# The bound of |v| as ScalarE sums in place of VectorE maxima, and column halves for the 90-row scores

## Chip, core and metric

The kernel runs on one core of a Trainium2 chip. The metric is device time in microseconds (us) of the whole program, less is better. The engines are TensorE (PE; PEld is its weight load), VectorE (DVE), ScalarE (ACT), GpSimd (POOL) and SyncE (SP), which issues most DMAs.

## What is computed

An attention with mixed heads, and a gated layer on its output. There are 4 batches, 12 heads, 448 tokens and a head width of 64; the layer has 1792 tokens, width 768 and an inner width of 1536.

```python
scores = scale * np.matmul(q, k.transpose(0, 1, 3, 2))
scores = np.einsum('bhij,hg->bgij', scores, w_pre)
scores = scores - np.max(scores, axis=-1, keepdims=True)
attn = np.exp(scores)
attn = attn / (np.sum(attn, axis=-1, keepdims=True) + 1e-09)
attn = np.einsum('bhij,hg->bgij', attn, w_post)
out = np.matmul(attn, v)
...
gate = 1.0 / (1.0 + np.exp(-(x @ w_gate)))
return gate * (x @ w_val) @ w_out
```

## The kernel before

The attention comes first, and the layer (the MoE part of the code) follows it. Queries are cut into blocks of 120, 120, 120 and 88 rows for each batch; the last is taken as 90 rows, since heads are mixed in sets of 10 rows. Two sets make a unit, and there are 92 units. The code is written out slot by slot, one slot for each unit, and every engine takes its instructions in that order.

In slot s, TensorE does, in this order: `premix` of unit s+2 (`pm`, L211), one `scores` call of a later block (`qk`, L157), `postmix` of unit s (`mx`, L253), and a part of `av` (L280, attention times v). ScalarE does the exponential of the first set (`e`, L223, an ACTIVATE and a read of its accumulator), the copy of one score tile (`st`, L163), the second exponential, then `mix` (L261, which empties the one `mx` buffer in PSUM, so that the `postmix` of slot s+1 waits for it), and in some slots `xt` (L290) or a sum over weights (L989). VectorE does a reciprocal (`ss`, L229, which waits for `ss` from GpSimd, L228), two row maxima (`nm`, L216), the other copy of the scores (L163), two `pl` (L241), and then what the plan adds to the slot. GpSimd does `ss`, two `ph` (L235), and in many slots a conversion of weights (L1067, L1075). Three slots take two `scores` calls, the second one at the slot's end: 13, 36 and 59, each just after six 90-row calls.

`scores` multiplies 64 rows of q and k for two heads, one head in each half of the array's rows. For a block of 120 query rows it cuts the columns at 64, so that four matmuls (each of them two instructions, for f32) have a quarter of the array each. For the 90-row blocks there is no cut. These are 6 calls for each of the four batches, 24 in all, in slots 7 to 12, 30 to 35, 53 to 58 and 76 to 81.

The layer scales its operands by powers of two, and needs a bound of |x|. It is the largest bound of |v| times the largest row sum of |w_post|. `v_max` (L175) gives one column of `vm` for each batch and head, by a VectorE reduction over 256 values in each partition; there are 48 of them, 12 for each batch, one for each slot from the batch's slot 6 on, with slots left out (`taken`) in which other VectorE work stands. `v_bound` (L181, L182 and the transpose L999) combines them after every second batch, and its result goes through SP's queue as `max_x`.

Of the kernel before, what the change touches and what calls it, by code (L numbers as in the profile page):

```python
# [9 lines left out]
F32 = mybir.dt.float32  # L10
F32R = mybir.dt.float32r
F16 = mybir.dt.float16
BF16 = mybir.dt.bfloat16
# [3 lines left out]
AF = mybir.ActivationFunctionType  # L17
ALU = mybir.AluOpType
AX = mybir.AxisListType
# [6 lines left out]
QUAD = 4  # L26
# [15 lines left out]
def _attention(ctx, tc, ins, B, H, S, D, xs, raws, make_moe):  # L42

    nc = tc.nc
# [11 lines left out]
    const = ctx.enter_context(tc.tile_pool(name="a_const", bufs=1))  # L56
# [32 lines left out]
    w2lo = const.tile([128, HK], F16, name="w2lo")  # L89
    sw = const.tile([128, 1], F32, name="sw")  # L90
    iw = const.tile([128, 1], F32, name="iw")
    vm = const.tile([128, B * H], F32, name="vm")
    vr = const.tile([128, 1], F32, name="vr")
    wr = const.tile([128, 1], F32, name="wr")
    wc = const.tile([128, H], F32, name="wc")
# [30 lines left out]
    moe = make_moe(NG)  # L126
# [23 lines left out]
    def scores(bi, c, sc):  # L150
        b, n = blocks[bi][0], R * blocks[bi][4]
        q, k = q_t[bi], k_t[b, c]
        cuts = [(0, 64), (64, n)] if n > 96 else [(0, n)]
        for s0, s1 in cuts:
            for e in range(2):
                rows = slice(64 * e, 64 * e + 64)
                nc.tensor.matmul(sc[e][s0:s1, :S], lhsT=q[rows, c, s0:s1], rhs=k[rows, :], start=True, stop=True)  # L157
# [8 lines left out]
    vt = {}  # L166
# [4 lines left out]
        vt[b, u] = t  # L171


    def v_max(b, h):
        nc.vector.tensor_reduce(vm[:, H * b + h:H * b + h + 1], vt[b, h // QUAD][:, h % QUAD].rearrange("p j d -> p (j d)"),  # L175
                                axis=AX.X, op=ALU.max, apply_absolute_value=True)

    def v_bound(b, step):
        g = "x", b // 2
        if step == 0:  # L180
            nc.vector.tensor_reduce(vr, vm[:, 2 * H * g[1]:2 * H * (g[1] + 1)], axis=AX.X, op=ALU.max)  # L181
            nc.vector.tensor_scalar(moe.one[("top",) + g], vr, wr, 1.001, op0=ALU.mult, op1=ALU.mult)  # L182
            stores.append(moe.flipped(g))
        else:
            moe.early_bound(g, step + 1)
# [112 lines left out]
    EARLY_AT = (5, 12, 19, 27, 34, 42, 49, 57)  # L298
# [3 lines left out]
    def at(slot, fn, *args):  # L302
        plan.setdefault(slot, []).append((fn, args))

    def spread(i, n, s0, s1):
        return s0 + i * (s1 - s0) // n

    taken = {EARLY_AT[k] + slot for k in range(moe.EARLY) for slot in (10, 11)}
    for b in range(B):
        f = first[PB * b]  # L310
        for u in range(NQ):
            at(f + 2 + 2 * u, v_load, b, u)
        s = f + 5
        for h in range(H):
            s = max(s + 1, f + 6 + 2 * (h // QUAD))
            while s in taken:
                s += 1
            at(s, v_max, b, h)
        if b % 2:
            at(s + 1, v_bound, b, 0)  # L320
        if b == 1:
            for step, slot in enumerate(BOUND[1:]):
                at(s + 1 + slot, v_bound, b, step + 1)
        for c in range(NP if b else 0):
            at(spread(c, NP, first[PB * (b - 1)] + 6, first[PB * b - 1] - LEAD - 2), k_load, b, c)
    for bi in range(1, NBK):
        s0, s1 = first[bi - 1] - LEAD, first[bi] - LEAD
        for c in range(NP):
            at(spread(c, NP, s0, s1), scores, bi, c)
        if bi > 1:  # L330
            at(s0 - 4, q_load, bi)
    for bi in range(NBK):
        s0 = first[bi + 1]
        s1 = first[bi + 2] if bi + 2 < len(first) else s0
# [39 lines left out]
    def ahead(c):  # L374
        if c % 3 == 0:
            mx = two_banks(ps_mx, "mx")
            sc = [mx[:, e] for e in range(2)]
        else:
            sc = pm[:2] if c % 3 == 1 else qk_banks()
        scores(0, c, sc)  # L380
        todo.append(sc)
# [14 lines left out]
    for s in range(min(min(plan), -LEAD), max(plan) + 1):  # L396
# [14 lines left out]
        def job(bi, c):  # L411
            sc = qk_banks()
            scores(bi, c, sc)
            return lambda e: keep(bi, c, e, sc)
# [785 lines left out]
@with_exitstack  # L1200
def kernel(ctx, tc, B, H, S, D, ins, out):
    nc = tc.nc
    top = ctx.enter_context(tc.tile_pool(name="top", bufs=1))
    dram = ctx.enter_context(tc.tile_pool(name="dram", bufs=1, space=DRAM))
    xs = dram.tile([B, H * D // 128, 128, S], F32, name="xs")
    with tc.manual_schedule():
        raws = top.tile([128, 13 * H * D // 2], F32, name="raws")
        with ExitStack() as c2:
            moe = _attention(c2, tc, ins, B, H, S, D, xs, raws,
                             lambda NG: _Moe(tc, xs, ins, out, raws, NG, top))  # L1210
        moe.run()
# [72 lines left out]
```

## Time and profile before

| what | value |
|---|---|
| median of 3 runs | 789.11 us (788.37 to 790.18) |
| profiled execution, first to last instruction (span) | 786.5 us |
| the median less that span | 2.6 us |
| mean granted TensorE clock | 0.998 |
| PE, DVE, ACT, POOL busy | 97%, 83%, 70%, 37% of the span |

The profiled execution's own time is given as its span; the 2.6 us beside it are the start and end of the program. The attention takes about the first 344 us. A slot is counted below from the first `mx` matmul of its unit to that of the next, so slot 8 is the stretch from 50.02 to 53.48 us.

### The profile page before, as it was taken

What the parts mean: (1) busy time and instruction counts of PE and PEld (TensorE: products, weight loads), DVE (VectorE), ACT (ScalarE), POOL (GpSimd) and SP (SyncE); (2) the same over time, 40 slices, a digit from 0 to 9 for tenths busy, and PEclk for the clock granted to TensorE, in tenths of its full rate; (3) what the DMA queues carried; (4) which work ended last, traced back from release to release, by engine and by line L of the source; (5) the groups of instructions that cost most, each with busy time, mean ns of one, the idle gap of its engine ahead of it and who ended that gap; (6) DMA issues with size and microseconds to landing.
All of it is one profiled execution on the core that took longest, in us unless ns stands there. A gap on an engine that the chain in (4) does not pass through costs nothing.

```text
span 786.5 us, 23288 instructions
## 1 busy us (share of the span) xinstructions
PE 760.4 (97%) x9530; PEld 417.6 (53%) x9530; DVE 649.4 (83%) x1116; ACT 548.3 (70%) x1058; POOL 293.7 (37%) x462
## 2 busy tenths in 40 slices
PE   7899999999999999888999999999999999999998
PEld 2455655565556555564555455555555555555554
DVE  4999999999989999999996989589876999997111
ACT  3887889788978888796875876577756784563000
POOL 1447776876786544410222222224222221010000
PEclk9999999999999999999999999999999999999999
DMA  5786568756875575839406284663567788995001
GB/s 183 232 255 223 192 231 260 252 193 227 284 261 186 183 226 186 250 105 321 143 27 224 92 301 152 251 222 141 198 205 263 277 313 312 383 346 206 36 36 70
DMA packets 80714, 166.13 MB, mean 211 GB/s; under 512 B 20448, under 2 KB 57664, under 8 KB 80608
## 3 DMA queue, kind: packets, MB, share of 16 engines
q1 hardware_dynamic: 72304, 132.88, 51.0%
q0 software_dynamic: 7728, 31.27, 10.3%
q8 instruction: 74, 1.21, 0.7%
q10 hardware_dynamic: 576, 0.51, 0.2%
q14 instruction: 32, 0.26, 0.1%
HBM read 87.77 MB, written 38.15 MB: 160 GB/s over the span
## 4 chain that ended last, share of the span: by engine, by line
PE 77%; ACT 9%; DVE 7%; DMA 3%; POOL 2%; issue 2%; SPq 0%; ACTq 0%; DVEq 0%; POOLq 0%
PE bank L1138 31%; PE bank L1149 18%; PE av L280 8%; PE pm L211 7%; PE qk L157 7%; PE mx L253 6%; ACT e L223 3%; ACT mix L261 2%; DVE nm L216 2%; DVE m L1122 2%; DMA k<-in_kp_dram 1%; ACT st L163 1%; ACT m L1117 1%; DVE m L1131 1%; DVE pl L241 1%
## 5 line engine op out<-in xcount | busy, mean ns | idle before, releaser
L1138 PEld LDWEIGHTS <-m 128*128 128x128 f16 x1512 | 147.5, 98 | 143.6 <-DVE m L1122 4.1
L1138 PE MATMUL bank<-m,m 128*128 128x448 f16 x1116 | 214.7, 352 | 4.6 <-DVE m L1122 3.2
L223 ACT ACTIVATE e<-pm,nm 128x448 f32<-128x448 f32 x180 | 115.2, 640 | 50.1 <-DVE nm L216 42.1
L235 POOL TENSOR_SCALAR ph<-e,ss 128x448 f16<-128x448 f32 x180 | 113.2, 641 | 55.3 <-DVE ss L229 31.3
L241 DVE SCALAR_TENSOR_TENSOR pl<-e,ss,ph 128x448 f16<-128x448 f32 x180 | 123.6, 725 | 1.2 <-POOL ph L235 1.2
L1149 PEld LDWEIGHTS <-m 128*128 128x128 f16 x756 | 74.0, 98 | 69.0
L216 DVE TENSOR_REDUCE nm<-pm 128x1 f32<-128x448 f32 x180 | 103.0, 613 | 7.2 <-PE pm L211 5.4
L253 PEld LDWEIGHTS <-ph 64*128 64x128 f16 x2880 | 67.6, 93 | 68.0 <-issue 34.5
L261 ACT ACTIVATE mix<-mx 128x960 f32<-128x960 f32 (+1 forms) x92 | 103.0, 1119 | 0.0
L157 PE MATMUL qk<-k,q 64*64 64x448 f32 (+2 forms) x640 | 94.9, 545 | 4.4 <-ACT st L163 2.8
L211 PE MATMUL pm<-T,w 64*64 64x448 f32 (+1 forms) x720 | 95.3, 560 | 1.3 <-ACT e L223 0.7
L280 PE MATMUL av<-mix,v 128*64 128x120 f32 (+1 forms) x1504 | 92.6, 267 | 1.4 <-ACT xt L290 1.4
L1149 PE MATMUL bank<-m,m 128*128 128x448 f16 x468 | 92.9, 352 | 0.0
L1075 POOL CAST raws<-raws 128x768 f16<-128x768 bf16 x36 | 40.6, 1127 | 117.4 <-ACT raws L1069 117.4
L253 PE MATMUL mx<-w2hi,ph 64*128 64x60 f16 x1440 | 70.9, 188 | 9.3 <-ACT mix L261 8.9
L1138 PE MATMUL bank<-m 128*128 128x448 f16 x396 | 77.9, 353 | 0.0
L280 PEld LDWEIGHTS av<-mix,v 128*64 128x64 f32 x1504 | 73.5, 137 | 6.2 <-ACT xt L290 1.7
L253 PE MATMUL mx<-w2hi,pl 64*128 64x60 f16 x1440 | 70.4, 187 | 0.2 <-DVE pl L241 0.2
L253 PE MATMUL mx<-w2lo,ph 64*128 64x60 f16 x1440 | 70.5, 187 | 0.0
L1165 DVE TENSOR_TENSOR m<-bank,m 128x448 f32<-128x448 f32 x72 | 44.4, 619 | 22.1 <-PE bank L1138 13.9
L253 PEld LDWEIGHTS <-pl 64*128 64x128 f16 x1440 | 61.7, 93 | 0.3 <-DVE pl L241 0.3
L228 POOL TENSOR_SCALAR ss<-ss 128x2 f32<-128x2 f32 (+1 forms) x92 | 30.2, 328 | 81.4 <-ACT e L223 79.0
(124 smaller groups left out, 1079.3 us busy)
## 6 DMA issues: line engine op xcount, KB each, us to landing
T<-st SPq DMA_DIRECT2D x176, 210.0 KB
m<-w SPq DMA_DIRECT2D x60, 384.0 KB
raws<-in_w_dram SPq DMA_DIRECT2D x28, 767.6 KB
hs<-m POOLq DMA_DIRECT2D x48, 224.0 KB, 3.2
m<-hs SPq DMA_DIRECT2D x15, 672.0 KB
w<-m POOLq DMA_DIRECT2D x21, 384.0 KB, 4.7
w<-raws POOLq DMA_DIRECT2D x20, 384.0 KB, 4.5
v<-in_vb_dram SPq DMA_DIRECT2D x12, 512.0 KB
```

The costliest lines, as they stand in the source:

```text
L157: nc.tensor.matmul(sc[e][s0:s1, :S], lhsT=q[rows, c, s0:s1], rhs=k[rows, :], start=True, stop=True)
L211: nc.tensor.matmul(pm[bank][64 * x:64 * x + 64, :S], lhsT=w1[rows], rhs=T[rows, x], start=True, stop=True)
L216: nc.vector.tensor_reduce(nm[:, i:i + 1], pm[bank][:, :S], axis=AX.X, op=ALU.max, negate=True)
L223: nc.scalar.activation(out=e_t[u][:, i], in_=pm[units[u][2][i]][:, :S], func=AF.Exp, bias=nm_t[u][:, i:i + 1], scale=1.0, accum_out=ss_t[u ...
L235: nc.gpsimd.tensor_scalar(ph[:, i], e_t[u][:, i], ss_t[u][:, i:i + 1], 1.0, op0=ALU.mult, op1=ALU.mult)
L241: nc.vector.scalar_tensor_tensor(pl[:, i], e_t[u][:, i], ss_t[u][:, i:i + 1], p_t[u][0][:, i], op0=ALU.mult, op1=ALU.subtract)
L253: nc.tensor.matmul(mx[:, x, i, jb * HK:(jb + 1) * HK], lhsT=p[rows, i, JB[jb]:JB[jb] + 128], rhs=w[rows], start=(k == 0), stop=(k == 2))
L261: nc.scalar.activation(out=out.rearrange("p g (y r) -> p y g r", r=HALF), in_=mx_t.pop(u), func=AF.Copy, scale=1.0 / (P_UP * W_UP))
L280: nc.tensor.matmul(av_t[bi][64 * i:64 * i + 64, c % 4, :n], lhsT=vt[b, u][:, h + i, jb, :], rhs=mixes[bi % 2][:, jb, 2 * c + i, :n], start ...
L1138: self.nc.tensor.matmul(self.f32(bank), lhsT=w[a][:, k], rhs=x[b][:, k], start=self.START[i] and k == r == 0, stop=k == self.KH - 1 and r ...
L1149: self.nc.tensor.matmul(self.f32(bank), lhsT=w[a][:, k], rhs=b[bb], start=self.START[i] and j == k == r == 0, stop=j == OUT_TILES - 1 and ...
L1165: self.nc.vector.tensor_tensor(self.f32(out), self.f32(bank), self.f32(snap), op=ALU.add)
```

## The change

Three things are changed. The 48 reductions of VectorE become 24 ACTIVATEs of ScalarE with the function Abs, each over the 512 values of two heads, whose accumulator gives a sum (an upper bound of the maximum); the absolute values go to a scratch tile. They stand in six slots for each batch (6 to 11; 29 and 32 to 36; 52 and 55 to 59; 75 to 80), between the second exponential and `mix`. Since a batch has six of them, `v_bound` stands in slot 37 and slot 81, where it was in slots 47 and 87. The 90-row `scores` are cut at column 64 like the others.

```diff
-    vm = const.tile([128, B * H], F32, name="vm")
+    vm = const.tile([128, B * H // 2], F32, name="vm")
+    v_abs = const.tile([128, 2 * 4 * D], BF16, name="v_abs")
...
-        cuts = [(0, 64), (64, n)] if n > 96 else [(0, n)]
-        for s0, s1 in cuts:
+        for s0, s1 in ((0, 64), (64, n)):
...
-    def v_max(b, h):
-        nc.vector.tensor_reduce(vm[:, H * b + h:H * b + h + 1], vt[b, h // QUAD][:, h % QUAD].rearrange("p j d -> p (j d)"),
-                                axis=AX.X, op=ALU.max, apply_absolute_value=True)
+    def v_sum(b, i):
+        v = vt[b, 2 * i // QUAD][:, 2 * i % QUAD:2 * i % QUAD + 2].rearrange("p h j d -> p (h j d)")
+        nc.scalar.activation(out=v_abs, in_=v, func=AF.Abs, accum_out=vm[:, H // 2 * b + i:H // 2 * b + i + 1])
...
-            nc.vector.tensor_reduce(vr, vm[:, 2 * H * g[1]:2 * H * (g[1] + 1)], axis=AX.X, op=ALU.max)
+            nc.vector.tensor_reduce(vr, vm[:, H * g[1]:H * (g[1] + 1)], axis=AX.X, op=ALU.max)
...
-    taken = {EARLY_AT[k] + slot for k in range(moe.EARLY) for slot in (10, 11)}
+    taken = {EARLY_AT[k] + slot for k in range(moe.EARLY) for slot in (11, 12)}
...
-        for h in range(H):
-            s = max(s + 1, f + 6 + 2 * (h // QUAD))
+        for i in range(H // 2):
+            s = max(s + 1, f + 6 + 2 * (2 * i // QUAD))
             while s in taken:
                 s += 1
-            at(s, v_max, b, h)
+            at(s, v_sum, b, i)
```

The order of ScalarE in slots 9 and 10 before, from the first copy of slot 9 on (`e,ss` is the exponential and its sum, `mix` empties `mx`, `xt` empties `av`):

```order
L163 COPY st<-qk 90x448
L223 ACTIVATE e,ss<-pm_117,nm 128x448
L261 ACTIVATE mix_168<-mx 128x4x48x5
L290 ACTIVATE xt<-av,sw 128x480
L223 ACTIVATE e,ss<-pm_115,nm 128x448
L163 COPY st<-qk 90x448
L223 ACTIVATE e,ss<-pm_116,nm 128x448
L261 ACTIVATE mix_168<-mx 128x4x48x5
```

The same place with the change (L176 is the new sum):

```order
L163 COPY st<-qk 90x448
L223 ACTIVATE e,ss<-pm_117,nm 128x448
L176 ACTIVATE v_abs,vm<-v 128x512
L261 ACTIVATE mix_169<-mx 128x4x48x5
L290 ACTIVATE xt<-av,sw 128x480
L223 ACTIVATE e,ss<-pm_115,nm 128x448
L163 COPY st<-qk 90x448
L223 ACTIVATE e,ss<-pm_116,nm 128x448
L176 ACTIVATE v_abs,vm<-v 128x512
L261 ACTIVATE mix_169<-mx 128x4x48x5
```

Each sum stands ahead of the `mix` of its slot, and so ahead of `xt` and of the next slot's exponentials.

The order of VectorE near the end of the attention before, in slots 87 and 88 (L181, L182 and L999 are `v_bound`, L1131 combines tiles for the layer):

```order
L241 SCALAR_TENSOR_TENSOR pl<-e,ss,ph 128x448 x2
L181 TENSOR_REDUCE vr<-vm 128x1
L182 TENSOR_SCALAR one_x_163<-vr,wr 128x1
L999 STREAM_TRANSPOSE junk<-one_x_163 128x32
L1131 TENSOR_TENSOR m_7971<-m_7971 128x768 x2
L229 RECIPROCAL ss<-ss 128x2
L216 TENSOR_REDUCE nm<-pm_115 128x1
```

The same place with the change:

```order
L241 SCALAR_TENSOR_TENSOR pl<-e,ss,ph 128x448 x2
L1131 TENSOR_TENSOR m_8002<-m_8002 128x768 x2
L229 RECIPROCAL ss<-ss 128x2
L216 TENSOR_REDUCE nm<-pm_115 128x1
L216 TENSOR_REDUCE nm<-pm_116 128x1
```

The three steps of the bound are gone from here; they stand six slots earlier, and the DMA of `max_x` with them.

## Rows read from the trace of the kernel before

**Rows 1.** The page, part 1: busy us (share of the span) and instructions.

```profile
PE 760.4 (97%) x9530; PEld 417.6 (53%) x9530; DVE 649.4 (83%) x1116; ACT 548.3 (70%) x1058; POOL 293.7 (37%) x462
```

**Rows 2.** Windows of slots 8, 15, 13: length, busy us (instructions) of PE, PEld, DVE, ACT, POOL.

```profile
50.02:53.48 3.46, 3.46 (x78) 2.06 (x76) 3.27 (x8) 2.79 (x6) 1.58 (x4) 1.00 0.85 227
75.67:79.07 3.40, 3.40 (x84) 2.03 (x81) 3.40 (x9) 3.24 (x7) 2.41 (x4) 1.00 0.20 73
67.27:72.27 5.00, 4.70 (x93) 2.40 (x90) 5.00 (x10) 3.43 (x8) 2.98 (x6) 1.00 0.82 253
```

**Rows 3.** Chain that ended last, slots 8 and 16: start us, us, what.

```profile
49.26 0.92 PE qk L157 x4
50.18 0.66 PE mx L253 x48
...
78.39 0.75 PE qk L157 x8
79.14 0.77 PE mx L253 x48
```

**Rows 4.** Timeline of ScalarE, slots 8 to 10; in brackets idle time and releaser.

```profile
51.76 1.13 ACT L261 ACTIVATE mix<-mx 128x960 f32<-128x960 f32 x1
...
56.20 0.65 ACT L290 ACTIVATE xt<-av,sw 128x480 f32<-128x480 f32 x1
57.03 0.63 ACT L223 ACTIVATE e<-pm,nm 128x448 f32<-128x448 f32 x1 [0.18 <-DVE nm L216]
```

**Rows 5.** A group by form: count, busy us, mean ns, idle before.

```profile
L989 ACT ACTIVATE junk<-m 128x448 f16<-128x448 f32 x48 | 27.6, 574 | 24.3 <-DVE m L1171 14.2 <-DMA max_w<-junk 5.9 <-DVE m L1165 3.5
```

**Rows 6.** Timeline of ScalarE, a sum of 384 and its follower.

```profile
85.60 0.55 ACT L989 ACTIVATE raws<-raws 128x384 f16<-128x384 f32 x1
...
86.10 0.66 ACT L223 ACTIVATE e<-pm,nm 128x448 f32<-128x448 f32 x1
```

**Rows 7.** Chain that ended last, slots 81 and 82.

```profile
313.05 1.03 ACT mix L261
...
314.13 0.84 PE mx L253 x48
```

**Rows 8.** Windows of slots 34 to 36, and of 56 to 59: the sums.

```profile
sum 12.71, PE 12.08 PEld 6.71 DVE 10.91 ACT 9.25 POOL 10.24; mean PE 4.03 PEld 2.24 DVE 3.64 ACT 3.08 POOL 3.41
...
sum 17.90, PE 16.05 PEld 9.06 DVE 15.20 ACT 12.08 POOL 14.83; mean PE 4.01 PEld 2.26 DVE 3.80 ACT 3.02 POOL 3.71
```

**Rows 9.** Timeline of GpSimd, slots 33 to 36.

```profile
140.10 0.37 POOL L228 TENSOR_SCALAR ss<-ss 128x2 f32<-128x2 f32 x1
...
142.23 2.44 POOL L1067 TENSOR_SCALAR raws<-raws 128x384 int16<-128x384 int8 x1
...
150.46 1.21 POOL L1067 TENSOR_SCALAR raws<-raws 128x384 int32<-128x384 int16 x1
```

**Rows 10.** Timeline of VectorE, slots 33 and 34.

```profile
140.35 0.41 DVE L175 TENSOR_REDUCE vm<-v 128x1 f32<-128x256 f32 x1
140.68 0.15 DVE L229 RECIPROCAL ss<-ss 128x2 f32<-128x2 f32 x1
...
142.34 1.27 DVE L241 SCALAR_TENSOR_TENSOR pl<-e,ss,ph 128x448 f16<-128x448 f32 x2
...
144.98 0.17 DVE L229 RECIPROCAL ss<-ss 128x2 f32<-128x2 f32 x1 [1.05 <-POOL ss L228]
```

**Rows 11.** Chain that ended last, slot 59.

```profile
235.52 0.38 ACT st L163
...
235.95 1.20 PE qk L157 x6
```

**Rows 12.** Timeline of VectorE, slot 87.

```profile
330.15 0.17 DVE L181 TENSOR_REDUCE vr<-vm 128x1 f32<-128x24 f32 x1
...
330.74 1.91 DVE L1131 TENSOR_TENSOR m<-m 128x768 f32<-128x768 f32 x2
```

**Rows 13.** Waits of SP's queue, 300 to 350 us: total, times, longest.

```profile
SPq L269 <- DVE junk L999: 2.7, 1, 2.7
```

## The prediction

> **What bounds the kernel now.** The page's first part comes first: TensorE is busy for 97% of the span [rows 1], so a change gains where it shortens TensorE's slots or a wait of TensorE, and loses where it makes one. The windows by slot show which of the two applies. Slot 8 (with a 90-row call) takes 3.46 us and TensorE is busy for all of it; slot 15 (with a 120-row call) takes 3.40, and is full too [rows 2]. Slot 13 takes 5.00 us with two calls [rows 2]; a full slot of this kind would be 3.40 and the second call's 0.75 [rows 2, 3], 4.15 us, so 0.85 are lost there. By the same count slots 34 to 36 should take 2 x 3.40 + 4.15 = 10.95 and take 12.71, and slots 56 to 59 should take 14.35 and take 17.90 [rows 8]: 1.76 and 3.55 us are lost. Everywhere else in the stretches that the change touches TensorE is the bound, or the two-slot loop in which a `mix` frees the buffer of the next `postmix`: in slots 81 and 82 `mix` starts at 313.05, ends after 1.03, and `postmix` starts at 314.13, 0.05 later [rows 7].
>
> **The 90-row scores.** The cut adds 24 pairs of matmuls and takes none away. In the chain an uncut call takes 0.92 us, and the `postmix` behind it 0.66; a cut one of 120 rows 0.75, and its `postmix` 0.77 [rows 3]. So 0.17 us are gained in the call and 0.11 given back behind it, 0.06 net, which is what the slots show (3.46 against 3.40 [rows 2]). The second half of 26 columns has no row; it is taken as the 56 columns of the 120-row blocks. Over 24 calls that is at most 1.4 us. Eighteen calls stand in slots that also get a sum, or next to a stall, and gain nothing there (below); six (slots 12, 30, 31, 53, 54, 81) keep it: **-0.4 us** (bounds 0 and -1.4).
>
> The Trainium skill (TensorEngine Tiling (Array Packing), Key Properties) says that different tiles load weights and multiply in parallel. By that alone the cut would be worth the whole 0.17 us a call, 24 x 0.17 = 4.1 us; the rows speak for 0.06.
>
> **The sums on ScalarE.** No row shows 512 values. One of 448 takes 574 ns [rows 5]. One of 384, with the read of its accumulator, keeps ScalarE for 0.50 us, from 85.60 to 86.10 [rows 6]. From 448 to the 960 values of a `mix` (1.13 us [rows 4]) an element costs (1130 - 574) / 512 = 1.1 ns, so 128 more than 384 make 0.14: I take 0.64 us for each, bounds 0.50 and 1.13. The function Abs stands between exponentials already, so I count no load of tables.
>
> What hides it is the idle time ahead of `postmix`. In slot 8 `mix` ends at 51.76 + 1.13 = 52.89, and the next `postmix` starts at 53.48 [rows 2, 4]; less the 0.05 of the handover the cover is 0.54 us. The sum stands ahead of `mix`, so 0.64 is 0.10 too much, once in each loop of two slots: slots with a sum take 3.51 instead of 3.46, and the gain of the cut is gone in them. Where `xt` (0.65 us [rows 4]) stands in the slot, the exponential behind it has only 0.18 us of idle time [rows 4], so it starts 0.46 late, and everything behind it too. In batch 0 that is 5 x 0.05 + 0.46 = 0.7, less some 0.1 that slots already waited: **+0.6**; in batch 3, with the same six slots, **+0.6**. In batch 1 it is one such `xt` (slot 32), **+0.4** (0 if the stall behind it takes it up). In batch 2 the stall of slots 56 to 58 takes it up.
>
> In slots 36 and 59 the sum delays more: behind `mix` stands the copy of the second call. In slot 59 this copy starts at 235.52 and ends 0.38 later, and the next `scores` call starts at 235.95 [rows 11]. So the whole sum lands on TensorE: **+0.6** in slot 59, and **+0.45** in slot 36, where the copy may also wait for TensorE (bounds 0 and 0.64 each).
>
> **The maxima taken from VectorE.** Each takes 0.41 us [rows 10], 48 of them. In full slots VectorE waits for TensorE and the gain is nothing; TensorE's own work covers it. In the stalled slots it can count. In slot 33 `ss` of GpSimd ends at 140.10 + 0.37 = 140.47, and the reciprocal starts at 140.68, behind a maximum that began at 140.35 [rows 9, 10]: 0.2 us late. What is late next is `ph`, then the conversion of weights on GpSimd. The one at 142.23 takes 2.44 us, twice the 1.21 of the one at 150.46 [rows 9], and lies over two `pl` of 1.27 us in all [rows 10]; VectorE then waits 1.05 us for GpSimd [rows 10]. So the loss is GpSimd's, and the maximum is not in it, unless an earlier reciprocal lets the conversion get ahead of `pl`. I take half of the losses at slot 13 (**-0.4**, bounds 0 and -0.85), a third at slots 34 to 36 (**-0.6**, bounds 0 and -1.76), and only the one maximum of 0.4 at the entry to slots 56 to 59, where the chain repeats itself (**-0.5**, bounds 0 and -3.55).
>
> The Trainium skill (Advanced Engine Details and Errata, VectorE Performance Modes) says that VectorE's second SBUF port is shared with GpSimd, and that each blocks the other when VectorE uses both. A maximum reads one tensor and is no such case by that rule; the rows agree in so far as the 2.44 us are about 1.21 and the 1.27 of two `pl`.
>
> **The earlier bound.** At 330.15 the three steps of `v_bound` begin, and the next instruction, on the chain, starts at 330.74 [rows 12]. Without them it can start 0.59 us earlier, if its tiles are there: **-0.4** (bounds 0 and -0.59). SP's queue waited 2.7 us there for the transpose [rows 13], with reads of x behind it; those are issued earlier, and I count nothing for them, since the term already lets all of VectorE's work move up. Six slots earlier the same 0.59 stands where a maximum of 0.41 is gone, with VectorE waiting for TensorE; in slot 37 it is covered by the maxima that are gone from the slots behind it. If that cover failed, each would cost 0.59.
>
> **Sum.** -0.4 + 0.6 + 0.6 + 0.4 + 0.6 + 0.45 - 0.4 - 0.6 - 0.5 - 0.4 = +0.35 us on the profiled execution, whose span is 786.5 us, 2.6 below the median of the runs. With 789.11 that is **789.5 us**.
>
> **Rivals.**
> *GpSimd's stalls go.* If the earlier reciprocals let the conversions pass ahead of `pl`, all of 1.76 and 3.55 comes back, 4.2 us more than I count: 785.3; with the second stretch alone 786.4. For it: VectorE is on time 0.2 us earlier [rows 9, 10]. Against it: VectorE waits for GpSimd in the stall, not the other way round [rows 10].
> *Late `mix`, and nothing from VectorE.* The stalls are GpSimd's alone and stay, the bound's tiles are not there earlier, and the sums cost their full price. Both `xt` of a batch then pass on 0.46, so 0.25 + 0.9 = 1.15 in each of three batches, 1.1 in slots 36 and 59, less 0.4 for the cut: +4.1, 793.2; with the stall of batch 1 taking up its part, 792.0. The point from which it decides is a sum of more than 0.54 us [rows 2, 4].
> *The cut gives its whole 0.17 us in each call*, and the sums are hidden: 789.5 - 3.7 = 785.8. Against it stands the longer `postmix` [rows 3].
> *Nothing changes that counts.* If a sum takes 0.50 us it fits under the 0.54, and all terms but the cut and the bound shrink: 788.7.
>
> **How the numbers follow.** A measurement of this kernel tells 0.2%, 1.6 us, from no change. The forecast has 0.45, the fourth case 0.10 (both within 0.2%), the late `mix` 0.24 (slower), the freed GpSimd 0.17 and the full cut 0.04 (faster). The range from 786.4 to 792.0 leaves out about a tenth at each end; the forecast's own range is 788.2 to 790.8. Faster 0.21, same 0.55, slower 0.24.
>
> **What would show it.** Slots 9 and 78 about 0.5 us longer, and slots with a sum near 3.50; slots 12, 30, 31 at 3.40; in slots 36 and 59 the second copy 0.6 us later; sums of 0.6 us between exponential and `mix`. Conversions of 2.4 us in slots 34 and 56 to 58 say that the stalls stay; 1.2 to 1.6 us there would make the prediction wrong on the fast side. Waits for `mix` of over 0.3 us in every slot with a sum would make it wrong on the slow side.

## The result, and the profile after

The change makes the kernel slower: 801.07 us (median of 4 runs, 800.94 to 802.14) against 789.64 us for the kernel before in the same session. The ratio is 1.0148, with a 95% interval of 1.0134 to 1.0162. By the ratio that is 11.7 us (by the two medians 11.4), and the forecast was 789.5 us with a range up to 792.0. The span of the profiled execution goes from 786.5 to 800.4 us.

The first part of the page after answers to [rows 1] (busy us, share of the span, instructions):

```profile
PE 778.9 (97%) x9626; PEld 418.8 (52%) x9626; DVE 638.3 (80%) x1068; ACT 566.1 (71%) x1106; POOL 292.6 (37%) x462
```

TensorE is busy for 18.5 us more, with only 96 records more; VectorE has lost 11 us and ScalarE gained 18. So most of the time isn't a new wait of TensorE: TensorE itself takes longer. The windows of slots 8, 13 and 15 answer to [rows 2] (length; busy us and instructions of PE, PEld, DVE, ACT, POOL; granted clock, DMA share, GB/s):

```profile
51.78:56.04 4.26, 4.26 (x83) 2.15 (x82) 3.13 (x6) 3.51 (x9) 1.92 (x3) 1.00 0.85 223
72.21:76.60 4.39, 4.39 (x92) 2.34 (x88) 3.83 (x9) 3.27 (x8) 2.07 (x5) 1.00 0.82 254
80.01:83.41 3.40, 3.40 (x84) 2.03 (x81) 3.40 (x9) 3.24 (x7) 2.27 (x4) 1.00 0.08 24
```

Slot 8, with a 90-row call, took 3.46 us and takes 4.26, full of TensorE's work, at the same granted clock (1.00, the 2.4 GHz level). Slot 15, with a cut 120-row call, is where it was. Slot 13, 5.00 us before, has lost its stall. The chain that ended last shows where the 0.80 us sits, and answers to [rows 3] (start us, us, what):

```profile
53.59 0.91 PE pm L211 x8
54.50 1.61 PE qk L157 x8
56.10 0.77 PE mx L253 x48
```

The call (`qk`) takes 1.61 us, where the uncut one took 0.92 and the cut one of 120 rows 0.75; the `postmix` (`mx`) behind it takes 0.77 in place of 0.66. That is 0.69 + 0.11 = 0.80 us a call. The instructions by form in the stretch 59.3 to 60.2 us, inside the next call, show why (count; shortest, median and longest ns; first and last start us; forms):

```profile
L157 PE MATMUL qk<-k,q x6: 534/536/555, 59.0 to 59.8; 64*26 64x448 f32 x4, 64*64 64x448 f32 x2
L157 PEld LDWEIGHTS qk<-k,q x4: 98/100/101, 59.4 to 59.5; 64*26 64x26 f32 x4
```

The call begins at 58.57. (Each matmul in f32 leaves two records.) The weights of the pieces of 26 columns are loaded only from 59.4 us on, when the last of the 64-column ones, started at 59.0 with 0.54 us each, is nearly through. The two widths run one after the other.

By slot, the span's 13.9 us are made up as follows. The 24 slots with a 90-row call (6 to 11, 29 to 34, 52 to 57, 75 to 80) give +17.9: 24 x 0.795 = 19.1 (the slots grow by 0.79 to 0.80), less some 2.1 in slots 29, 34, 56 and 57, which held stalls that the longer call now covers, and 0.9 more in slot 7, a gap of a kind whose place and size change from one execution to the next (run 8). Four stalls outside them shrink (slots 13, 35, 58, 59: -0.60, -0.75, -0.30, -1.17), slot 36 grows by 0.48, slots 47 to 51 lose 0.56, slot 88 loses 0.55 and slot 90 grows by 0.77. The stretch ahead of slot 0 and that from slot 91 on are together 1.3 shorter.

### The profile page after: what moved, and what is told of

It is laid out like the page before. It is cut to its first block, busy times and chain, and to the rows that moved or that the text cites. A ratio compares the mean times of both kernels' runs of the same rounds, so it can differ in the third digit from the quotient of the medians.

```text
span 800.4 us, 23490 instructions
## 1 busy us (share of the span) xinstructions
PE 778.9 (97%) x9626; PEld 418.8 (52%) x9626; DVE 638.3 (80%) x1068; ACT 566.1 (71%) x1106; POOL 292.6 (37%) x462
## 4 chain that ended last, share of the span: by engine, by line
PE 84%; ACT 7%; DVE 5%; DMA 1%; issue 1%; POOL 1%; SPq 0%; ACTq 0%; DVEq 0%; POOLq 0%
PE bank L1138 34%; PE bank L1149 18%; PE qk L157 9%; PE av L280 9%; PE pm L211 7%; PE mx L253 6%; ACT e L223 3%; DVE nm L216 2%; ACT mix L261 1%; DVE pl L241 1%; ACT st L163 1%; ACT m L1117 1%; DVE m L1122 1%; DMA k<-in_kp_dram 1%; DVE st L163 0%
## 5 line engine op out<-in xcount | busy, mean ns | idle before, releaser
L241 DVE SCALAR_TENSOR_TENSOR pl<-e,ss,ph 128x448 f16<-128x448 f32 x180 | 120.8, 710 | 1.2 <-POOL ph L235 1.2
L157 PE MATMUL qk<-k,q 64*64 64x448 f32 (+1 forms) x736 | 112.6, 541 | 2.1 <-ACT st L163 2.1
L253 PEld LDWEIGHTS <-ph 64*128 64x128 f16 x2880 | 64.6, 93 | 73.6 <-POOL ph L235 33.3
L1075 POOL CAST raws<-raws 128x768 f16<-128x768 bf16 x36 | 37.6, 1045 | 119.3 <-ACT raws L1069 119.3
L228 POOL TENSOR_SCALAR ss<-ss 128x2 f32<-128x2 f32 (+1 forms) x92 | 37.4, 407 | 101.2 <-ACT e L223 99.6
L163 DVE COPY st<-qk 120x448 f32<-120x448 f32 (+1 forms) x92 | 56.8, 618 | 13.5 <-PE qk L157 13.1
```

The lines of the kernel that those rows point to most:

```text
L163: (nc.vector.tensor_copy if e else nc.scalar.copy)(st_t[bi][:n, 2 * c + e], sc[e][:n, :S])
L241: nc.vector.scalar_tensor_tensor(pl[:, i], e_t[u][:, i], ss_t[u][:, i:i + 1], p_t[u][0][:, i], op0=ALU.mult, op1=ALU.subtract)
L253: nc.tensor.matmul(mx[:, x, i, jb * HK:(jb + 1) * HK], lhsT=p[rows, i, JB[jb]:JB[jb] + 128], rhs=w[rows], start=(k == 0), stop=(k == 2))
```

## The experiments

Three theories stood at the start. **N**: a second piece of at most 32 columns doesn't run beside one of 64, and the rest of the change costs next to nothing. **S**: the sums on ScalarE delay `mix` in the loop. **M**: the added matmuls cost by their number. All runs are compared with the kernel before on the same chip, at 788.33 us median for runs 1 to 4, 789.0 for runs 5 to 8, and 789.1 for run 9.

**Run 1, the sums alone.** The changed kernel without the cut:

```
-        for s0, s1 in ((0, 64), (64, n)):
+        cuts = [(0, 64), (64, n)] if n > 96 else [(0, n)]
+        for s0, s1 in cuts:
```

> The change without the cut: 90-row scores are uncut, the sums on ScalarE and the earlier bound stay. Theory N (the narrow piece of 26 columns does not run beside the one of 64 but after it, about 0.79 us for each of 24 calls): the slots with 90-row calls are back near 3.46 to 3.5 us, and the time is 801.1 - 18.9 = 782 plus what the stalls of slots 13, 34 to 36 and 56 to 59 still cost (up to 6 us): 783 to 789. Rival S (the sums ahead of mix make the slots long, as the prediction's slower case has it, at a higher price): slots with a sum stay near 4.26, and the time near 801.

Measured: 790.12 us, ratio 1.0019 (0.9997 to 1.0041). S falls: the sums with the moved bound bring at most 3.2 of the 11.7 us, and perhaps nothing. N's own range was missed by 1.1 us.

**Run 2, the cut alone.** The kernel before with the opposite of that edit.

> The kernel before with the cut alone. Theory N: all 24 slots with 90-row calls take 4.2 to 4.3 us, the time is 789.6 + 18.9 less up to 6 us of stalls that the longer slots hide: 802 to 808. Rival S: no slower than before, 788.5 to 790.

Measured: 801.63 us, ratio 1.0162 (1.0146 to 1.0178). The whole loss is the cut's; the time is 0.4 us below the range that N gave. The windows of its slots 9, 36 and 59:

```profile
55.45:59.70 4.25, 4.25 (x82) 2.14 (x80) 3.37 (x7) 3.39 (x8) 1.92 (x3) 1.00 1.01 244
156.47:160.86 4.39, 4.39 (x92) 2.32 (x89) 4.16 (x10) 3.28 (x8) 2.30 (x4) 1.00 0.86 239
241.09:245.48 4.39, 4.39 (x92) 2.31 (x89) 4.35 (x11) 3.29 (x8) 2.67 (x5) 1.00 0.83 261
```

**Runs 3 and 4, a second piece of 33 and of 32 columns.** The kernel before, cut, with the second piece widened past the block's end; the scores of the added columns are not read. Run 4 has 96 where run 3 has 97; the lines that load the added columns of q are left out here.

```
-        cuts = [(0, 64), (64, n)] if n > 96 else [(0, n)]
-        for s0, s1 in cuts:
...
+        for s0, s1 in ((0, 64), (64, n if n == QB else 97)):
...
```

> The kernel before with the cut, the second piece widened from 26 to 33 columns; the 7 more columns are other columns of q or zeros, and their results are not read. Theory N, if what counts is that 26 columns fit a column group of 32: at 33 the pieces run side by side as in the 120-row blocks, slots with 90-row calls take 3.40, the time is 788 to 789.6. Rival M (eight matmuls with eight weight loads cost more than four, whatever their width): as the cut alone, 802 to 808.

> As the run with 33 columns, but with 32. Theory N with a border at 32: as the cut alone, slots of 4.26, 802 to 808. If the border lies lower, between 26 and 32, or if the match to the wider piece is gradual: near the run with 33 columns, or between. Rival M: as the cut alone too, and so this run separates only together with the one of 33.

Measured: 789.84 us, ratio 1.001 (0.9993 to 1.0028) with 33 columns; 801.7 us, ratio 1.0163 (1.0146 to 1.018) with 32. One column makes 11.9 us. The number of matmuls is the same in both, so M falls (it had 802 to 808 for both). The times lie 0.2 us above and 0.3 below N's ranges. The chain of run 3, then that of run 4:

```profile
52.37 0.75 PE qk L157 x8
53.13 0.77 PE mx L253 x48
```

```profile
54.04 1.61 PE qk L157 x8
55.65 0.77 PE mx L253 x48
```

With 33 columns the call takes the 0.75 us of the 120-row one, and the slot 3.40; with 32 it takes 1.61, and the slot 4.26.

**Run 5, three narrow pieces.** What was open then: is it the narrow piece that is slow (T), or the change of width inside a call (W)?

```
-        cuts = [(0, 64), (64, n)] if n > 96 else [(0, n)]
-        for s0, s1 in cuts:
+        for s0, s1 in ((0, 64), (64, n)) if n > 96 else ((0, 32), (32, 64), (64, n)):
```

> The kernel before, with the 90 columns of a call cut into 32, 32 and 26: six matmuls of at most 32 columns, none of 64. It does the whole computation. Run 2 had slots of 4.26 us with 64 and 26. If a narrow piece just can't run beside a piece of 64 columns (theory W), the six run beside each other as one group, the call costs what a cut 120-row call does and the slots with a 90-row call go back to 3.40 to 3.5 us: 787 to 790 us. If every narrow piece takes its own turn, whatever stands beside it (theory T), there are two more turns than in run 2, each some 0.8 us: slots near 5 us or above and 815 us or more. If only the pieces with other column strips of the same mode overlap partly, it lies between.

Measured: 789.08 us, ratio 1.0011 (0.9995 to 1.0028). The chain:

```profile
52.11 0.89 PE qk L156 x12
53.00 0.77 PE mx L252 x48
```

Six matmuls of 32, 32 and 26 columns take 0.89 us together. Narrow pieces run beside each other, so T falls.

**Run 6, one head after the other.** The kernel before with the cut; in a 90-row call the order is 64, 26, 64, 26 columns.

```
-        cuts = [(0, 64), (64, n)] if n > 96 else [(0, n)]
...
+        cuts = ((0, 64), (64, n))
+        order = [(e, cut) for cut in cuts for e in range(2)] if n > 96 else [(e, cut) for e in range(2) for cut in cuts]
...
+            for e, (s0, s1) in order:
```

> The kernel before with the cut of 64 and 26 columns, but in the 90-row calls both pieces of the first head are issued ahead of both pieces of the second: 64, 26, 64, 26 where run 2 had 64, 64, 26, 26. Same matmuls, same computation. If each change of width ends a group that runs side by side (theory W), there are four groups instead of two, two more at about 0.8 us each in 24 calls: slots of 5.4 to 5.9 us in place of 4.26, 830 to 840 us. If the price of 0.8 us belongs to the narrow pieces as such, one turn for both (theory T), the order doesn't matter: 801 to 802 us.

Measured: 843.62 us, ratio 1.0703 (1.0681 to 1.0725). The chain, and the window of one slot:

```profile
57.89 3.35 PE qk L158 x8
61.24 0.77 PE mx L254 x48
```

```profile
61.17:67.17 6.00, 6.00 (x83) 2.45 (x82) 3.37 (x7) 3.52 (x7) 1.44 (x3) 1.00 0.30 102
```

The same four matmuls take 3.35 us, four turns of 0.84. In run 2 they took 1.61, two turns of 0.80; in run 3 0.75, one turn. That is W, with a price of about 0.86 us for each further turn (1.61 - 0.75; 3.35 - 1.61 = 1.74 for two). The time was some 4 us above the range that W gave, since each turn had been put at 0.8.

**Run 7, the whole change with 33 columns.** The edit of run 3 in the changed kernel.

> The changed kernel whole (sums, bound, cut), but the second piece of a 90-row call has 33 columns in place of 26; the seven added columns are the next block's or zeros, and nothing reads their scores. It is the change as the prediction costed it, with a second piece like that of 56 columns. The prediction's terms give 0.35 us over before; by runs 1 (sums alone, 1.0019) and 3 (cut of 33 alone, 1.001) it is 0 to 2.5 us over before, 788.3 to 791. If the sums and the cut each only uncover stalls that the other uncovers too, it stays under 1 us over before. Far from that, 800 us, would mean that narrowness isn't what made the changed kernel slow.

Measured: 790.07 us, ratio 1.0015 (0.9999 to 1.0032). This is the kernel that the prediction costed: its terms give +0.35 us, and the run shows +1.2 (-0.1 to +2.5). No experiment points to a version that beats the kernel before.

**Run 8, the kernel before once more.** Unchanged, for a second profile.

> The kernel before once more, unchanged, for a second profile: it shows by how much the slots of one execution differ from those of another. Slots full of TensorE's work should agree within 0.05 us; the stalls at slots 13, 35, 59, 60 and the slots 81 to 90 are the question. If they differ by what runs 1 and 3 showed there (0.3 to 2.7 us), the differences of those runs in such slots say nothing of the change.

Measured: 788.36 us, one run; span 786.6 us against 786.5. Most full slots agree within 0.05 us. Others don't: slot 8, full before, is 0.94 longer, slot 35 0.65, slot 50 0.47, slot 58 0.69, slot 59 0.70 shorter, slot 90 0.76 longer. The window of slot 8, and TensorE's timeline in it:

```profile
50.13:54.54 4.41, 3.69 (x79) 2.06 (x77) 3.28 (x8) 2.78 (x6) 2.16 (x4) 1.00 0.82 221
```

```profile
52.44 0.43 PE L280 MATMUL av<-mix,v 128*64 128x120 f32 x4 [0.72 <-issue]
```

TensorE stops for 0.72 us in the middle of an `av`, and "issue" says that it waited for nothing that the chain shows. Run 7 has such a gap of 2.00 us in its slot 56, and one of 1.61 in its slot 7. Behind that one the granted clock was lower: slot 7 takes 6.72 us there, with TensorE busy for 5.11 at a mean granted clock of 0.75 (3.4 us of it at the 1.2 GHz level), and so 3.26 more than before. So a difference of 1 us in one slot of one execution says little by itself, and the +0.77 of slot 90 is not the change's: the kernel before takes 2.84 us there in one profile and 3.60 in the other.

What these gaps have in common can be read from the traces. The first line below is the end of run 7's gap, the second the DMA queue `q8` of the kernel before (packets, MB, share of the engines):

```profile
226.73 0.84 PE L281 MATMUL av<-mix,v 128*64 128x120 f32 x12 [2.00 <-issue]
q8 instruction: 74, 1.21, 0.7%
```

A packet of `q8` is 16 KB, and there are 74 to 76 for the some 19,100 to 19,500 records of TensorE and its weight loads: one for 256 records. Nine gaps over 0.35 us in the attention, in seven of the profiles, are put down to "issue", or, in slot 7 of the changed kernel and of run 7, to a VectorE instruction that was long done or that the stopped matmul doesn't read. Ahead of each of the nine stands a number of records that leaves 193 over when it is divided by 256, and TensorE goes on 1.37 to 1.55 us after a packet of `q8` has landed (run 8: landed 51.02, on at 52.44; run 7: 225.30 and 226.73). So the likely cause is that TensorE waits there for its own next instructions. Run 8's gap stands behind 1473 records and the two in slot 7 behind 1217, one step of 256 earlier: which of these places becomes a gap differs from one execution to the next. What makes such a packet late was not tried.

**Run 9, the control for run 6.** The order of run 6 with the 33 columns of run 3.

> Run 3 (second piece of 33 columns, the seven added ones unread) with the order of run 6: 64, 33, 64, 33, one head after the other. It is the control for run 6, whose 843.62 us could be the order's and not the widths'. If a change between the two widths ends a group that runs side by side (theory W), 64 and 33 are no such change, the four matmuls run together in this order too, the call takes about 0.75 us and the time is 788 to 791 us. If the order itself keeps the four apart (the two heads read different rows of the array, the two pieces write different columns), it comes near run 6, 820 us or above.

Measured: 790.42 us, ratio 1.0024 (1.0008 to 1.004). The window of slot 9:

```profile
52.72:56.12 3.40, 3.40 (x84) 2.02 (x82) 3.27 (x9) 3.25 (x7) 1.58 (x4) 1.00 0.83 225
```

3.40 us, as in run 3: the order alone costs the slot nothing, and run 6's price is that of the change between widths. Why the whole is 0.1 to 0.4% above before stays open; in the profiled execution slots 12 and 32 are 1.6 and 1.4 us longer.

## Why the prediction was wrong

**The step that failed** is one sentence of the part on the 90-row scores: "The second half of 26 columns has no row; it is taken as the 56 columns of the 120-row blocks." With 56 columns, or 33 (run 3), four matmuls run side by side in 0.75 us. With 26 or 32 (runs 2 and 4) the second pair waits for the first, and a call takes 1.61. The term of -0.4 us is +19.1 in its 24 slots, of which the stalls and the ends of the span gave some back.

The prediction had no upper bound for this term: it went from 0 to -1.4, as if a cut could at worst do nothing. The rows of before had one. If two pairs don't overlap, the call takes two turns of 0.75 us [rows 3] in place of one of 0.92, and its `postmix` 0.11 more: +0.69 a call, 16.6 us in all. That was a rival on the slower side, with a place and a price, and it wasn't among those of the prediction.

The Trainium skill has a rule that speaks for it. TensorEngine Tiling (Array Packing), Key Properties, says beside the rule cited in the prediction that changing the tiling mode, and not just the tile, drains the TensorE. The Trainium skill, under the same title, Tiling Modes, lists tiles of 64 rows by 64 columns and of 64 by 32. If a piece of up to 32 columns uses the second and one of 33 to 64 the first, the rule fits what runs 2 to 6 and 9 show (0.75 us without a change of width, 1.61 with one, 3.35 with three); no trace names the mode, so that reading is an inference. The prediction took the rule on parallel tiles from that section and left the one on modes.

**The other steps**, read where the cut doesn't cover them (run 7), or against run 2, which differs from the changed kernel by the sums and the bound alone:

- *The length of a sum.* Taken as 0.64 us. ScalarE's timeline after, in slot 8:

```profile
52.93 0.62 ACT L176 ACTIVATE v_abs<-v 128x512 bf16<-128x512 f32 x1
53.45 0.20 ACT L176 ACTIVATION_READ_ACCUMULATOR v_abs<-v 128x1 f32 x1
53.54 1.12 ACT L261 ACTIVATE mix<-mx 128x960 f32<-128x960 f32 x1
```

From the sum's start to `mix` it is 0.61 us: right.

- *Batches 0 and 3, +0.6 each.* In run 7 slots 75 to 80 take 21.20 us together against 20.79, +0.41; in run 1, without the cut, they are 0.50 longer. Slots 75, 76 and 79 of run 7:

```profile
291.32:294.92 3.60, 3.47 (x85) 2.11 (x82) 3.24 (x8) 3.47 (x10) 2.01 (x5) 1.00 0.86 253
294.92:298.33 3.41, 3.41 (x81) 2.03 (x80) 3.08 (x8) 3.36 (x8) 1.44 (x4) 1.00 0.81 263
...
305.33:309.12 3.79, 3.48 (x85) 2.11 (x82) 3.54 (x10) 3.79 (x10) 1.59 (x4) 1.00 0.48 158
```

Every second slot is longer by TensorE's idle time, and in slot 79 ScalarE is busy for all of its 3.79 us. Mechanism right, size a little high; the long slots are 10 and 79 (+0.3), where the prediction named 9 and 78. Batch 0 of both runs also holds a gap of the kind in run 8, so its sum isn't a price. For batch 1 the prediction had +0.4; slots 32 and 33 are 0.37 longer in run 1 and 0.45 in run 7. In the changed kernel the sums cost nothing there: those slots take 4.26 with them and 4.26 without (run 2), presumably since a longer call gives `mix` more room. The rival of the late `mix` fell with that; without the longer call it had 1.15 us for batch 3, where runs 1 and 7 show 0.50 and 0.41.

- *Which slots.* The prediction named slots 12 and 81 among those with a 90-row call. By the windows, in which the prediction reads them, they hold none: slot 12 takes 3.40 before and after. In the written order the call of slot s stands ahead of its `postmix`, and so in the window of slot s-1. The 24 calls are in the windows 6 to 11, 29 to 34, 52 to 57 and 75 to 80, and all but four of these (30, 31, 53, 54) also hold a sum, where the prediction counted six.

- *Slots 36 and 59, +0.45 and +0.6.* Against run 2 they grow by 0.48 and 0.29. The windows after:

```profile
157.09:161.97 4.88, 4.38 (x93) 2.22 (x90) 4.15 (x9) 4.39 (x11) 2.67 (x5) 1.00 0.82 254
241.93:246.61 4.68, 4.37 (x88) 2.21 (x87) 4.39 (x9) 4.13 (x10) 2.77 (x5) 1.00 0.75 233
```

The sum stands ahead of `mix` and of the second copy, and TensorE idles 0.50 and 0.31 us: right in the first, half in the second.

- *Slot 13, -0.4 (0 to -0.85).* It loses 0.60 in the changed kernel, and then TensorE is busy for all of it: a full slot of this kind is 4.39 us, not the 4.15 that the prediction counted (slot 36 before takes 4.39 too, all of it TensorE's). So the losses before were 0.61, 1.52 and 3.31 us, not 0.85, 1.76 and 3.55. But runs 2 and 3 lose the same 0.60 with all maxima in place. The maxima aren't needed for it, and what ends the stall isn't settled.

- *Slots 34 to 36 and 56 to 59, -0.6 and -0.5 from VectorE.* The sums of these windows after answer to [rows 8]:

```profile
sum 12.54, PE 12.04 PEld 6.41 DVE 9.84 ACT 10.99 POOL 7.62; mean PE 4.01 PEld 2.13 DVE 3.28 ACT 3.66 POOL 2.54
...
sum 16.81, PE 16.38 PEld 8.55 DVE 13.31 ACT 14.17 POOL 10.03; mean PE 4.09 PEld 2.14 DVE 3.33 ACT 3.54 POOL 2.51
```

They are 0.17 and 1.09 us shorter although three of the seven slots carry a longer call (+0.80 each). GpSimd's busy time in the second falls from 14.83 to 10.03 us, and its conversions take 1.2 us, not 2.4:

```profile
237.81 1.22 POOL L1067 TENSOR_SCALAR raws<-raws 128x384 int32<-128x384 int16 x1
242.13 1.22 POOL L1067 TENSOR_SCALAR raws<-raws 128x384 int32<-128x384 int16 x1
```

The prediction named 1.2 to 1.6 us there as the sign that these stalls go. The long conversions do go: those of slots 56 to 58 take 0.8 to 1.2 us in runs 1 and 7 too, and 2.1 to 2.4 in run 8. But they take 0.8 to 1.2 us in run 2 as well, with all maxima in place, so in the changed kernel the longer call alone could have done it. The first rival wanted the conversions to be short, and with them all of the lost time back. In slots 56 to 59 part of it comes back: they are 2.06 us shorter in run 1, and 0.41 in run 7 in spite of the gap of 2.00; but also 1.59 in run 2 and 0.56 in run 8. And it is lost again just ahead: slots 52 to 59 together are 1.6 us longer than before in run 1 and 0.3 in run 7, against 0.6 shorter in run 8. TensorE's timeline of run 1 shows one place where it is lost:

```profile
220.92 0.97 PE L212 MATMUL pm<-T,w 64*64 64x448 f32 x4 [1.22 <-DMA T<-st]
```

TensorE waits there for the transfer of `T`. Run 3 has the same wait (1.12 us) without any sum, so the sums aren't its cause; whether earlier conversions make it likelier was not tried. In the changed kernel the longer calls cover it. At slots 34 to 36, 0.63 of the 1.52 us that were lost before was no stall of GpSimd's, but a gap of TensorE of the kind in run 8:

```profile
143.71 0.98 PE L211 MATMUL pm<-T,w 64*64 64x448 f32 x8 [0.63 <-issue]
```

- *The earlier bound, -0.4 (0 to -0.59).* Slot 88 takes 4.45 us in place of 5.01:

```profile
345.01:349.46 4.45, 3.20 (x68) 2.00 (x68) 4.42 (x8) 2.41 (x6) 1.73 (x3) 1.00 1.11 316
```

It loses 0.55 to 0.57 us in the changed kernel and in runs 1 and 7, and 0.01 or less in all other runs: right, and near its full price.

- *A term that was missing.* The first bound has left slots 47 and 48. The window of slot 47 before, and after:

```profile
188.33:191.84 3.51, 3.26 (x85) 1.97 (x82) 3.44 (x12) 3.21 (x8) 2.15 (x4) 1.00 0.78 263
```

```profile
196.34:199.54 3.20, 3.20 (x86) 1.89 (x82) 3.20 (x9) 3.13 (x8) 2.23 (x5) 1.00 0.82 244
```

VectorE had twelve instructions there and was all but full; with nine, TensorE is full instead. Slots 47 to 51 are 0.56 to 0.58 shorter in the changed kernel and in runs 1 and 7, and 0.03 or less in runs 2, 3, 5, 6 and 9. The prediction asked what the first bound costs where it goes, and not what it frees where it was.

- *The sums of the rivals.* The third rival calls the sums hidden, but its 785.8 us still holds the 2.65 that the prediction counted for them; by its own words it would be 783.1.

Run 7 puts the sum of all this at +1.2 us (-0.1 to +2.5), where the prediction had +0.35. Several smaller terms were misread, as said, and partly made up for one another; the term that was set by a like-looking form, with no row of its own, was off by 19.5 us, and it decided the result.

## What to carry to other kernels

Before a matmul is cut into pieces, ask whether the pieces are of a kind that the trace shows running side by side; a form without a row gets a price on the slower side too, that of pieces one after the other. Where an odd rest is left, pad it (33 columns in place of 26 made 11.8 us here, runs 2 and 3) or cut all pieces narrow, and don't alternate the widths. Neither of the two was faster here than no cut. A second profile of the kernel before costs one run, and shows which slots' differences mean anything.

## What the runs showed of the hardware

Pieces of 26 or 32 columns of weights did not run beside pieces of 64, and pieces of 33 or 56 did; 32, 32 and 26 ran beside each other. Each change between the two kinds inside a call cost about 0.86 us with 448 moving columns in f32: calls of 0.75, 1.61 and 3.35 us for none, one and three changes. An uncut call of 90 columns is followed by a `postmix` of 0.66 us, one of any cut by 0.77; that fits a price for the change of kind as well, since `postmix` has weights of 64 by 128 itself, but no run tested it. TensorE also stood still for 0.4 to 2.0 us at places that differ between executions of like kernels, each a multiple of 256 of its records from the others and 1.37 to 1.55 us behind a packet of the instruction queue: most likely a wait for its own instructions (run 8).
